# A fused attention and feed-forward kernel: adding transfers issued behind GpSimd's second long product, and new places for the pieces of the preparations

## The chip, the cores and the metric

The kernel runs on one core of a Trainium2 chip. The metric is the time of one execution on the device, in microseconds (us). The core has TensorE (PE, matrix products; PEld is its loading of weights), VectorE (DVE), ScalarE (ACT), GpSimd (POOL) and SyncE (SP, which only starts transfers here). GpSimd computes and also starts those transfers that add to what lies at their destination; writing out the descriptors of such a transfer keeps GpSimd busy.

## What is computed

Attention over pooled keys, and a feed-forward layer behind it:

```python
kv_pool = kv.reshape(B, H // r, r, W // r, r, C).mean(axis=(2, 4))   # r = 4
k = v = kv_pool.reshape(B, -1, C) @ w_sr                             # 768 keys
a = softmax((q @ k.T) / sqrt(C))
x = a @ v                                    # B = 4, N = 12288, C = 128
h = x @ w_in                                 # d_ff = 2048
out = (h - tanh(h)) @ w_out
```

Every output element of 4 x 12288 x 128 in float32 is wanted.

## The kernel before

The queries go in groups of 512: 24 groups in each of 4 batches, 96 in all. A group has an attention part (`attention`) and a feed-forward part (`feed_forward`). The attention is written about the centre of a batch's keys, so that only what lies beyond a linear term needs exp: three tiles of scores (line 774), E = exp of them (778, ScalarE), r2 = E - 1 - s (781, VectorE). The three r2 of a group are added into one tile rs by transfers: a plain copy from SP (794) and two adding transfers that GpSimd starts (797). The sum of rs gives the shares (802), den; the values (818) and three products of the straight term (808) give num; df = num x t (829) is rounded to dr (832, GpSimd), and what the rounding left is dl (858, GpSimd). ql (812, GpSimd) is the same for q.

The feed-forward part takes dr through eight pairs of products with a scaled w_in (889). For seven of the eight the cubic term is one square on ScalarE (893) and one operation on VectorE (896). For the first of the eight, GpSimd does it: ScalarE copies (900), GpSimd adds 1 (903) and multiplies twice (907): first z = z x v, then rp = z x v. These are GpSimd's two long products. The products with Wr (927) gather all eight and the slope's term (878) in acc, and line 938 copies the result out.

The order is not written out line by line. Each operation is given to a planner (`Plan`) with a step, an engine, a duration and the tiles that it reads and writes. A step is an eighth of a group (UN = 8), so that group g's feed-forward starts at step 8g. The places within a group are in the table AT; `more` = [6.92, 9.07] are the two long products. Operations marked `lane` keep the order of their steps on their engine. All others go where the planner's own simulation has them ready, the one with the lowest step first. Tiles with one tag share a ring of buffers in the order of the tiles' steps. The PSUM bank "x" is such a ring with one buffer: den, num and most of the small products of the preparations pass through it one after the other, with den at 0.46 and num at 1.98 modulo 8.

Ahead of batches 1 to 3 lies a preparation:

- The gathering: the 16 places of the pooling window are added into kvp (768 keys for each of 128 channels, 384 KB a transfer). SP loads the first (368), GpSimd starts the 15 others as adding transfers (366), one in each group. `GATHER` says how many groups before the batch's first group this begins.
- `keys`: partial sums of kvp on VectorE (428), their mean (432), the centre (440, 443), then kvp times w_sr twice (447, 456), the second moment (473) and its norm (346). They are `apart_by` steps apart.
- `about_centre`: the hidden layer at the centre (536, 541), a chain of small operations on GpSimd (561 to 592), and twelve pieces on GpSimd: four that scale winT for the slopes (678), four for Wr (698) and four that scale w_in (636). The slopes' products are at 685, in bank x. The tuples EARLY (batches 0 and 1) and LATER (2 and 3) hold their distances in steps: FS of the first products, CS of the chain's parts, AS of the slopes and the Wr pieces, APART from a slopes piece to its product, SA, TA and WI the starts of slopes, Wr and w_in, and WS the distance of the w_in pieces. Batch 0 reads none of the values that are changed.

Of the kernel before, what the change touches and what calls it, by code (L numbers as in the profile page):

```python
# [156 lines left out]
def attention_then_ffn(ctx: ExitStack, tc: tile.TileContext, q, kv_by_key, kv_by_place, w_sr, w_in,  # L157
                       w_out, out):
    nc = tc.nc
    V, A, PL, PE, SP = nc.vector, nc.scalar, nc.gpsimd, nc.tensor, nc.sync  # L160
# [5 lines left out]
    KH, UN, AN = K // 2, FT // 2, KT // 2  # L166
    NG = N // G
# [7 lines left out]
    plan = Plan(tc)  # L175
# [7 lines left out]
    def sb(key, tag, shape, dt=F32, step=-1e6):  # L183
        n = BUFS[tag]
        plan.tile(key, tag, n, lambda: wk.tile(shape, dt, tag=tag, name=tag, bufs=n), step)
# [169 lines left out]
    def keys(b, s0):  # L355

        kvp, row, cen, kTr, vv32, vvr, Mn = (
            f"{x}.{b}" for x in ("kvp", "row", "cen", "kTr", "vv32", "vvr", "Mn"))
# [4 lines left out]
        for w in range(W if b else 0):  # L363
            def gather(w=w):
                if w:
                    PL.dma_start(out=plan[kvp], in_=kv_by_place[b - 1, w], accum_op=ALU.add)
                else:
                    SP.dma_start(out=plan[kvp], in_=kv_by_place[b - 1, w])

            at = (b * NG - GATHER[b - 1] + max(w - 1, 0)) * UN + AT["more"][0] - 2 * UN  # L370
            plan.op(at - (0.01 if w else 4), *(("POOL", 0.87) if w else ("SP", 0.5)), gather, (), (kvp,),
                    late=3.0, dma=1.0, lane=w > 0)
        for j in range(0 if b else NK):
            gap = 0.1
# [2 lines left out]
            at = slice(j * KB, (j + 1) * KB)  # L377
# [24 lines left out]
        sb(Mn, "Mn", [P, C])  # L402
        Mh = f"Mh.{b}"
        sb(Mh, "Mh", [P, 2, C], R32)
        apart_by = (1, 5.3, 8, 8)[b]
        s1, s2, s3, s4 = (s0 + n * apart_by for n in range(1, 5))
        s4 = s4 if b else 24.0
        for x, at in ((pc, s0), (pm, s3), (p4, s4)):
# [95 lines left out]
    def about_centre(b, s0):  # L504
# [12 lines left out]
        sb(Wr, "Wr", [P, FT, C], R32)  # L517
        FS, CS, AS, APART, SA, TA, WI, WS = EARLY if b < 2 else LATER
        first_at = [s0 + FS * n if b else s0 - 9.9 + n / 4 for n in range(4)]
# [86 lines left out]
        if b:  # L606
            plan.op(known, on, 2.2, first_order, (hb,), (hb, gg), late=MORE)
            plan.op(known + CS, on, 1.9, slopes_of, (hb,), (hb,))
# [62 lines left out]
        for n in range(NW):  # L671
# [27 lines left out]

            plan.op(slopes_at[n], "POOL", 1.1, by_first, (gg, "winT"), ((wg, 0),), late=MORE if b else 0.0)  # L700
            plan.op(slopes_at[n], "ACT", 0.2, beside, (gg,), ((wg, 1),), late=0.1)
# [26 lines left out]
    AT = dict(  # L728
        forth=[3.94, 1.06, 1.67, 5.41, 0.16, 6.02, 6.63, -0.46],
        first=[4.44, 1.51, 2.12, 5.84, 0.59, 6.45, 7.06, -0.02],  # L730
        then=[6.19, 2.26, 3.01, 6.54, 1.52, 7.28, 8.03, 0.77],
        back=[11.04, 6.93, 7.24, 7.85, 6.32, 8.76, 9.37, 5.71],
        scores=[-20.66, -21.57, -19.38], exps=[-20.16, -21.13, -18.94],
        beyond=[-19.46, -20.25, -18.25], values=[-3.75, -5.26, -4.35],
        more=[6.92, 9.07],
        copied=-18.59, added=[-15.50, -11.66],
# [122 lines left out]

        plan.op(s0 + AT["lower_left"], "POOL", 1.29, lower_left, (df, dr), (dl,), lane=True)  # L860

    EARLY = (2, 4.4, 5, 3.5, 8, 15, 22, 8)
    LATER = (4, 9, 9, 7, 16, 34, 31, 9)
    MORE = 2
    ON_POOL = (0,)

    def feed_forward(g, s0):
# [277 lines left out]
    start(-LEAD - 80)  # L1145
    weights(-LEAD - 50, -LEAD - 60)
    plan.tile("held", "held", 1, lambda: None)
    GATHER = (24, 30, 30)
    KEYS, ABOUT = 104, 96
    KEYS1, ABOUT1 = 61, 60  # L1150
    SL = 6
# [4 lines left out]
    for b in range(B):  # L1156
        first = b * NG * UN
        keys(b, first - LEAD - (40, KEYS1, KEYS, KEYS)[b])
        if b == 0:
            out_weights(-17.7, -LEAD - 46)  # L1160
        about_centre(b, first - LEAD - (30, ABOUT1, ABOUT, ABOUT)[b])
        for g in range(b * NG, (b + 1) * NG):
            attention(g, g * UN - (PRO[g] if g < 3 else 0))
# [19 lines left out]
def build(shapes):  # L1183

    import concourse.bacc as bacc

    nc = bacc.Bacc("TRN2", target_bir_lowering=False, num_devices=1)
    ins = [
        nc.dram_tensor(f"in_{n}_dram", s, mybir.dt.from_np(d), kind="ExternalInput").ap()
        for n, (s, d) in shapes.items()  # L1190
    ]
    b, c, n = shapes["q"][0]
    out = nc.dram_tensor(_OUT, (c, b * n), F32, kind="ExternalOutput").ap()
    with tile.TileContext(nc) as tc:
        attention_then_ffn(tc, *ins, out)
    return nc
# [31 lines left out]
```

## Time and profile before

| | before |
| --- | --- |
| median of 3 runs | 1312.98 us (1312.15 to 1314.66) |
| the profiled execution | 1312.51 us |
| its span, first to last instruction | 1310.7 us |
| TensorE busy | 1267.8 us (97%) |
| VectorE busy | 1221.1 us (93%) |
| ScalarE busy | 1196.2 us (91%) |
| GpSimd busy | 1142.7 us (87%) |
| GpSimd's adding transfers into kvp | 45, 44.2 us |
| TensorE's load for rp, waiting for GpSimd | 33.1 us in 47 waits |

The shares of busy time lie close together and are averages over stretches with different limits, so the profile is read group by group. In a row of the order of time the first number is the start, the second the duration, then engine, line, operation, destination and sources; in brackets stands how long the engine was idle before it and for whom. Rows merge neighbours of one kind (x3 is three of them). Durations of GpSimd's instructions overlap a little; their ends are what others wait for.

### The profile page before, as it was taken

How to read it: one execution, taken by the hardware profiler on the slowest of the kernel's cores; microseconds unless marked ns; L12 is line 12 of the kernel's file. 1: busy time of each engine (PE TensorE's matmuls, PEld its weight loads, DVE VectorE, ACT ScalarE, POOL GpSimd, SP SyncE). 2: the span in 40 equal slices, each digit the busy share in tenths (PEclk: the TensorE clock that was granted, in tenths of full speed). 3: DMA queues.
4: the chain of work that ended last, by engine and by line, in shares of the span. 5: the costliest groups of instructions: out<-in, count | busy, mean ns of one | idle time of the engine just before them, and what ended most of it. 6: DMA issues, size and time to landing. Idle time of an engine off the chain costs nothing.

```text
span 1310.7 us, 17375 instructions
## 1 busy us (share of the span) xinstructions
PE 1267.8 (97%) x5520; PEld 888.8 (68%) x5520; DVE 1221.1 (93%) x1201; ACT 1196.2 (91%) x1423; POOL 1142.7 (87%) x969
## 2 busy tenths in 40 slices
PE   5899999999999999999999999999999999999997
PEld 3666666776666667767666666776766767667665
DVE  7789999898999998999999999899999999899996
ACT  4689999898999998999999999899999999899995
POOL 3578999899999997999999998899988888888896
PEclk9899999999999999999999999999999999999999
DMA  9165666545666654345666664344344444344431
GB/s 354 47 122 128 139 133 143 111 116 127 135 136 137 139 121 110 104 122 117 134 138 139 133 137 114 92 120 114 96 107 111 107 105 109 93 107 105 110 86 37
DMA packets 82708, 158.47 MB, mean 121 GB/s; under 512 B 9936, under 2 KB 12112, under 8 KB 82608
## 3 DMA queue, kind: packets, MB, share of 16 engines
q0 software_dynamic: 33552, 66.99, 31.4%
q1 hardware_dynamic: 49056, 90.29, 19.4%
q8 instruction: 45, 0.74, 0.2%
q14 instruction: 55, 0.45, 0.1%
HBM read 57.93 MB, written 25.39 MB: 64 GB/s over the span
## 4 chain that ended last, share of the span: by engine, by line
PE 42%; POOL 40%; ACT 8%; issue 5%; DVE 3%; DMA 2%; POOLq 0%; SPq 0%; ACTq 0%; DVEq 0%
PE acc L927 12%; PE big L889 11%; POOL rp L907 10%; POOL z L907 10%; POOL rs L797 5%; PE big L774 5%; PE x L818 4%; POOL z L903 4%; ACT E L778 4%; POOL dr L832 3%; POOL ql L812 3%; PE acc L878 2%; PE x L808 2%; ACT v L900 2%; ACT o L938 2%
## 5 line engine op out<-in xcount | busy, mean ns | idle before, releaser
L896 DVE SCALAR_TENSOR_TENSOR r<-big,u 128x1024 fp32r<-128x1024 f32 x672 | 778.4, 1217 | 24.9 <-ACT u L893 23.7
L893 ACT ACTIVATE u<-big 128x1024 f32<-128x1024 f32 x672 | 662.0, 1035 | 35.2 <-PE big L889 24.5
L889 PE MATMUL big<-dr,winr 128*128 128x512 f32 x1536 | 510.0, 413 | 1.6 <-DVE r L896 0.7
L927 PE MATMUL acc<-r,Wr 128*128 128x512 f32 x1344 | 426.1, 409 | 0.6 <-DVE r L896 0.6
L781 DVE SCALAR_TENSOR_TENSOR r<-E,big 128x1024 f16<-128x1024 f32 x288 | 350.2, 1217 | 41.1 <-ACT E L778 37.8
L889 PEld LDWEIGHTS big<-dr,winr 128*128 128x128 f32 x1536 | 276.8, 188 | 95.6 <-DVE r L781 23.5
L778 ACT ACTIVATE E<-big 128x1024 f32<-128x1024 f32 x288 | 296.1, 1029 | 16.4 <-PE big L774 6.0
L927 PEld LDWEIGHTS acc<-r,Wr 128*128 128x128 f32 x1344 | 251.7, 188 | 64.7 <-DVE r L896 1.5
L907 POOL TENSOR_TENSOR rp<-z,v 128x1024 fp32r<-128x1024 f32 x96 | 272.8, 2841 | 0.2
L907 POOL TENSOR_TENSOR z<-z,v 128x1024 f32<-128x1024 f32 x96 | 247.6, 2579 | 4.3
L797 POOL DMA_DIRECT2D rs<-r x188 | 222.0, 1181 | 5.9 <-DVE r L896 3.3
L774 PE MATMUL big<-qr,kTr 128*128 128x512 f32 x576 | 197.9, 425 | 4.4 <-ACT qr L759 1.6
L818 PE MATMUL x<-r,vvr 128*128 128x512 f16 x576 | 174.9, 386 | 0.0
L812 POOL TENSOR_TENSOR ql<-q,qr 128x512 fp32r<-128x512 f32 x96 | 163.3, 1701 | 5.2 <-ACT qr L759 5.2
L858 POOL TENSOR_TENSOR dl<-df,dr 128x512 fp32r<-128x512 f32 x96 | 163.7, 1706 | 0.0
L832 POOL TENSOR_SCALAR dr<-df 128x512 fp32r<-128x512 f32 x96 | 66.6, 694 | 108.5 <-DVE df L829 106.4
L774 PEld LDWEIGHTS big<-qr,kTr 128*128 128x128 f32 x576 | 105.0, 190 | 45.9 <-DVE r L781 15.0
L903 POOL TENSOR_SCALAR z<-v 128x1024 f32<-128x1024 f32 x96 | 107.8, 1123 | 0.0
L900 ACT COPY v<-big 128x1024 f32<-128x1024 f32 x96 | 97.8, 1018 | 1.1 <-PE big L889 1.0
L818 PEld LDWEIGHTS <-vvr 128*128 128x128 f16 x576 | 33.5, 98 | 79.4 <-issue 79.1
L938 ACT ACTIVATE o<-acc,At 128x512 f32<-128x512 f32 x96 | 65.7, 684 | 21.6 <-PE acc L927 21.4
L927 PE MATMUL acc<-rp,Wr 128*128 128x512 f32 x192 | 73.8, 466 | 10.8 <-POOL rp L907 7.7
(184 smaller groups left out, 1007.0 us busy)
## 6 DMA issues: line engine op xcount, KB each, us to landing
rs<-r POOLq DMA_DIRECT2D x188, 256.0 KB, 3.9
q<-in_q_dram SPq DMA_DIRECT2D x96, 256.0 KB
out_dram<-o SPq DMA_DIRECT2D x96, 256.0 KB
rs<-r SPq DMA_DIRECT2D x94, 256.0 KB
kvp<-in_kv_by_place_dram POOLq DMA_DIRECT2D x45, 384.0 KB, 5.0
r<-in_kv_by_key_dram SPq DMA_DIRECT2D x6, 512.0 KB
kc<-inverse SPq DMA_DIRECT2D x12, 256.0 KB
u<-in_moe_w_in_dram SPq DMA_DIRECT2D x3, 512.0 KB
```

Of the source, the lines that this page charges most:

```text
L774: PE.matmul(out=half(plan[s], h), lhsT=plan[kTr][:, n * P : (n + 1) * P], rhs=plan[qr], start=True, stop=True)
L778: A.activation(out=plan[e], in_=plan[s], func=AF.Exp)
L781: V.scalar_tensor_tensor(out=plan[r], in0=plan[e], scalar=-1.0, in1=plan[s], op0=ALU.add, op1=ALU.subtract)
L797: PL.dma_start(out=plan[rs], in_=plan[r2s[k]], accum_op=ALU.add)
L812: PL.tensor_tensor(out=plan[ql], in0=plan[qs], in1=plan[qr].bitcast(F32), op=ALU.subtract)
L818: PE.matmul(out=plan[num], lhsT=plan[vvr][:, n], rhs=half(plan[f"r2.{g}.{k}"], h), start=(start and h == 0), stop=(stop and h == 1))
L858: PL.tensor_tensor(out=plan[dl], in0=plan[df], in1=plan[dr].bitcast(F32), op=ALU.subtract)
L889: PE.matmul(out=half(plan[hp], h), lhsT=plan[winr][:, f * P : (f + 1) * P], rhs=plan[dr], start=True, stop=True)
L893: A.activation(out=plan[u], in_=plan[hp], func=AF.Square)
L896: V.scalar_tensor_tensor(out=plan[r], in0=plan[hp], scalar=1.0, in1=plan[u], op0=ALU.add, op1=ALU.mult)
L907: PL.tensor_tensor(out=plan[to], in0=plan[x], in1=plan[y], op=ALU.mult)
L927: PE.matmul(out=plan[acc], lhsT=plan[Wr][:, 2 * n + h], rhs=half(plan[r], h), start=(start and h == 0), stop=(stop and h == 1))
```

## The change

```diff
-            at = (b * NG - GATHER[b - 1] + max(w - 1, 0)) * UN + AT["more"][0] - 2 * UN
-            plan.op(at - (0.01 if w else 4), *(("POOL", 0.87) if w else ("SP", 0.5)), gather, (), (kvp,),
+            at = (b * NG - GATHER[b - 1] + max(w - 1, 0)) * UN + AT["more"][1] - 2 * UN
+            plan.op(at + (0.01 if w else -4), *(("POOL", 0.87) if w else ("SP", 0.5)), gather, (), (kvp,),
                     late=3.0, dma=1.0, lane=w > 0)
...
-        apart_by = (1, 5.3, 8, 8)[b]
+        apart_by = (1, 6, 8, 8)[b]
...
-    EARLY = (2, 4.4, 5, 3.5, 8, 15, 22, 8)
-    LATER = (4, 9, 9, 7, 16, 34, 31, 9)
-    MORE = 2
+    EARLY = (2.5, 4.4, 4, 6, 8, 18, 24, 8)
+    LATER = (4, 6, 9, 7, 18, 30, 31, 7)
+    MORE = 2.5
...
-    GATHER = (24, 30, 30)
+    GATHER = (24, 29, 29)
```

The adding transfers into kvp get a step just behind the second long product in place of one just ahead of the first. The first load by SP moves by the same 2.15 steps. For batches 2 and 3 the gathering begins one group later. In the preparation of batch 1 the parts of `keys` lie 6 steps apart in place of 5.3, the first products 2.5 in place of 2, the slopes' pieces 4 in place of 5 and their products 6 behind them in place of 3.5, and the pieces for Wr and w_in begin 3 and 2 steps later. In batches 2 and 3 the chain's parts lie 6 apart in place of 9, the slopes begin 2 steps later, the Wr pieces 4 sooner, and the w_in pieces lie 7 apart in place of 9. MORE is the time that the planner adds behind two operations in its simulation. No instruction is added or taken away.

## Rows read from the trace of the kernel before

**Rows 1.** Windows, line 938 only: stretch, length, busy (instructions), clock, DMA share, GB/s.

```profile
98.90:237.10 138.20, 7.57 (x12) 1.00 0.63 135
352.30:478.00 125.70, 6.94 (x11) 1.00 0.63 137
627.10:790.40 163.30, 8.96 (x14) 1.00 0.64 137
963.20:1085.50 122.30, 6.85 (x11) 1.00 0.44 108
```

**Rows 2.** Order of time, one group with an adding transfer into kvp.

```profile
406.11 0.61 POOL L832 TENSOR_SCALAR dr<-df 128x512 fp32r<-128x512 f32 x1 [1.06 <-DVE df L829]
...
407.69 0.87 POOL L366 DMA_DIRECT2D kvp<-in_kv_by_place_dram  x1
...
411.27 3.02 POOL L907 TENSOR_TENSOR rp<-z,v 128x1024 fp32r<-128x1024 f32 x1
...
413.65 1.88 POOL L858 TENSOR_TENSOR dl<-df,dr 128x512 fp32r<-128x512 f32 x1
...
414.34 0.30 PEld L927 LDWEIGHTS acc<-rp,Wr 128*128 128x128 f32 x2 [0.60 <-POOL rp L907]
...
416.11 1.49 POOL L797 DMA_DIRECT2D rs<-r  x1
...
422.74 0.60 PE L802 MATMUL x<-rs,share 128*128 128x512 f16 x2
```

**Rows 3.** Order of time, one group without such a transfer.

```profile
1027.86 0.62 POOL L832 TENSOR_SCALAR dr<-df 128x512 fp32r<-128x512 f32 x1 [1.54 <-DVE df L829]
...
1032.58 2.69 POOL L907 TENSOR_TENSOR rp<-z,v 128x1024 fp32r<-128x1024 f32 x1
...
1035.67 0.81 PE L927 MATMUL acc<-rp,Wr 128*128 128x512 f32 x2
...
1039.21 0.39 PE L878 MATMUL acc<-dl,Ah 128*128 128x512 f32 x1
```

**Rows 4.** Waits, 352 to 478 us: who waited for whom, total, times, longest.

```profile
PEld acc L927 <- POOL rp L907: 5.8, 10, 0.6
DVE r L781 <- ACT E L778: 4.5, 10, 0.9
```

**Rows 5.** Windows: PE, PEld, DVE, ACT, POOL busy; then line 366 alone.

```profile
282.40:352.30 69.90, 66.15 (x297) 46.75 (x296) 63.32 (x61) 61.46 (x76) 69.90 (x58) 1.00 0.60 130
...
282.40:352.30 69.90, 7.67 (x5) 1.00 0.60 130
```

**Rows 6.** Windows of the preparations of batches 1 to 3, line 938 only.

```profile
237.10:352.30 115.20, 5.43 (x9) 1.00 0.53 122
490.30:627.10 136.80, 6.84 (x11) 1.00 0.47 113
802.70:938.70 136.00, 6.90 (x11) 1.00 0.42 105
```

**Rows 7.** Order of time at the end of batch 2's gathering.

```profile
486.70 2.69 POOL L907 TENSOR_TENSOR rp<-z,v 128x1024 fp32r<-128x1024 f32 x1
...
492.54 0.17 DVE L432 TENSOR_REDUCE row<-row 128x1 f32<-128x24 f32 x1
...
498.99 0.60 PE L802 MATMUL x<-rs,share 128*128 128x512 f16 x2
```

**Rows 8.** Tiles kvp (100 to 480 us) and rs (350 to 480): landings.

```profile
DMA to landing us min/median/max: 4.6/5.1/6.3
...
DMA to landing us min/median/max: 3.8/3.9/4.5
```

**Rows 9.** Order of time in batch 1's preparation: the straight term behind a slopes piece.

```profile
295.19 0.30 PEld L808 LDWEIGHTS x<-qr,Mh 128*128 128x128 f32 x2 [1.18 <-DVE At L692]
295.20 0.73 PE L808 MATMUL x<-qr,Mh 128*128 128x512 f32 x2 [0.74 <-DVE At L692]
```

**Rows 10.** The page's DMA queues: kind, packets, MB, share of 16 engines.

```profile
q0 software_dynamic: 33552, 66.99, 31.4%
```

## The prediction

> **What bounds the kernel now.** I first cut the span into groups of 512 queries by the start of the result copy of line 938, which stands once in each group. Three stretches in which GpSimd begins one adding transfer per group last 138.20 us for 11 periods, 125.70 for 10 and 163.30 for 13; a late stretch with no such transfer lasts 122.30 for 10 [rows 1]. That is 12.56 us a group with the transfer and 12.23 without. These 34 groups are the largest piece of the span that the change touches, so the question is what the 0.33 us are.
>
> The order of time of one such group answers it [rows 2]. Counting from the start of dr at 406.11: the transfer's issue is at +1.58, before the first long product, and the second long product rp ends at 411.27 + 3.02 = 414.29, which is +8.18. TensorE's weight load for line 927 starts at 414.34, having waited 0.60 us for rp. In a group without the transfer [rows 3] rp ends at 1032.58 + 2.69 = 1035.27, which is +7.41 from dr at 1027.86, and TensorE takes it at 1035.67, +7.81, with no wait named. So the transfer pushes rp back by 8.18 - 7.41 = 0.77 us, of which 7.81 - 7.41 = 0.40 is free and some 0.37 is not: the 0.33 of the period. The list of waits says the same of ten groups: TensorE's loads for rp 5.8 us, and behind them VectorE for E 4.5 us [rows 4], because the scores stand behind rp in TensorE's order. Without the transfer VectorE has no such idle time, its work fills the 12.23 us, and this is the floor of a group.
>
> **Adding transfers behind the second product.** Fifteen issues per batch for batches 1 to 3 are moved past z*v, the first rs issue and rp on GpSimd's queue; nothing is added or removed. Their step is 0.01 after rp and 1.57 before dl (lower_left), and the lane fixes that order. rp then ends at +7.41 again, 0.40 before TensorE wants it. What is late next? Behind the transfer stand dl, ql, the second rs issue and the next dr. Their start doesn't move: the transfer was ahead of them before. dl ends at 413.65 + 1.88 = 415.53, +9.42 [rows 2], and TensorE takes dl at +11.35 [rows 3]: 1.9 us spare. The second rs issue ends at 417.60, +11.49, and dr is wanted at +12.23: GpSimd still waits 0.7 us for VectorE. So in the steady groups I cost the move at nothing, with these 0.7 us as the cover; a further 0.7 us of GpSimd work in such a group would bring the loss back. Gain: 138.20 + 125.70 + 163.30 - 34 x 12.23 = **11.4 us**, bounds 6 (if half of the wait comes back elsewhere) and 11.4.
>
> **One group later for batches 2 and 3** (29 in place of 30). In the preparation of batch 1 GpSimd is full for 69.9 us on end with five issues in it [rows 5]; four of them stay, behind rp. One issue less is 0.8 us. The three preparations take 115.20 us for 8 periods, 136.80 for 10 and 136.00 for 10 [rows 6], so above the floor 17.4, 14.5 and 13.7 us. The third has no adding transfer in it, the second had two at its end, and these go: 14.5 - 13.7 = 0.8 us. Together **1.6 us**, bounds 0.5 and 2.
>
> **The end of the gathering gets tight.** The last transfer of batch 2 was issued ahead of group 30's first product; now it is behind rp of group 31, at about 489.1 of the old time [rows 7]. It lands 4.6 to 6.3 us after its issue, median 5.1 [rows 8], so at 493.7 to 495.4. The six partial sums (line 428, about 0.2 us each) and the mean, which stood at 492.54, need it: the mean moves to 495 to 497. The planner reckons with a landing 4.87 us after the issue (0.87 + 3.0 + 1.0 in the code) and puts these small operations accordingly, but VectorE and TensorE take their queues in order: if the transfer lands later, up to 6.3 - 4.9 = 1.4 us of VectorE's queue (the cubes, then TensorE, which waits for them) stand behind it. The group's shares, which need the same PSUM bank after the centre, are at 498.99 [rows 7], so 2 us remain for the centre. The same holds for batch 3. In batch 1 the last issue moves only behind group 12's rp, about 5.6 us later, and lands just before its sums' old place. Besides, partial sums that slipped into VectorE's idle time of a transfer group find none now. Loss: 0 to 1.4 for each of three batches and up to 0.3 for the sums; I take 0.5 each, **1.5 us**, bounds 0 and 4.
>
> **Places of the preparation's pieces.** In batch 1 the second slopes piece had a place, 131.5 + 5 = 136.5, which modulo 8 is 0.5: between the shares (0.46) and the straight term (1.98), which use the same bank x. TensorE idled 0.74 us there, its load 1.18 [rows 9]. The new places (129.5 + 6 + 4n: 7.5 and 3.5 modulo 8) lie outside. But the moment of batch 1 goes from 126.9 to 129.0, which is 1.0 modulo 8, inside: TensorE's 12 products are work anyway, ScalarE's copy behind them is not, and no row shows it in this place; by the wait at [rows 9] I bound its cost by 0 and 1.2 us and take 0.6, as its input is ready early, which the slopes' was not. With the rest of batch 1's excess over batch 3 (17.4 - 13.7 = 3.7 us, of which the issues explain some 0.8 already booked and four that stay some 3) this leaves **0.6 us** gain, bounds -2 and 2.5. In batches 2 and 3 the pieces come in another order (chain 3 and 6 steps sooner, Wr 4 sooner, slopes 2 later, first slopes at 3 in place of 1 modulo 8). TensorE and VectorE have that work to do in any order, and idle gaps before dr take the pieces as soon as they are ready; I take 0, bounds -1.5 and 1.5 for both together. If a piece falls before rp and finds no idle time, a 0.8 us transfer's price (0.33) or more comes back in that group alone.
>
> **Sum.** 11.4 + 1.6 - 1.5 + 0.6 = 12.1 us. The profiled execution took 1312.51 us, its span 1310.7 with 1.8 around it; it gives 1300.4. The median of the runs shown is 0.47 above that execution, so I say 1300.9.
>
> **Rivals.** (1) *The steady gain comes, the rest turns against it*: late landings at their upper bound (4), pieces at theirs (-3.5), no gain from the later start: 11.4 + 0.5 - 4 - 3.5 = 4.4, so 1308.5. For it: the 2 us left for the centre; against: bounds seldom meet. Chance 0.10. (2) *Another wait takes rp's place*, since the 0.40 us of spare time at rp and the 0.7 us at dr are thin and the second rs issue now has the transfer just ahead of it: half of the steady gain, 1312.9 - 6.4 = 1306.5. Against it: a group without the transfer runs the very same order to the end of rp. 0.06. (3) *The move changes nothing*: the wait named for rp is in truth one for VectorE, which is as full either way (0.99 of the floor). Then only the pieces count, 1312 to 1313. Against: the waits vanish together with the transfer. 0.03.
>
> (4) *Slower: the shares wait.* Adding transfers for kvp and rs go out on one software queue: 45 x 0.393 + 188 x 0.262 MB is the 66.99 MB of queue 0 [rows 10]. So far the first rs transfer ran behind kvp's, now the second does, and it has no further transfer to wait for it but the shares. It is issued at +10.0 [rows 2], 2.9 after kvp's new issue at +7.1, and the shares are at 422.74, +16.63, or +16.3 at the shorter period: 6.3 us. If it moved only once kvp has landed, it would land at 5.1 - 2.9 + 3.9 = 6.1 in the median, just in time, but 6.3 - 2.9 + 3.9 = 7.3 at worst. The point is a landing of kvp's over 5.3 us; with half the transfers 0.9 late, 45 groups lose 20 us and the 11.4 are gained: 1312.9 + 9 = 1322. Against it: rs transfers issued 2.97 us behind kvp's land in 4.5 us at most, 3.9 in the median [rows 8]. Chance 0.03. The Trainium skill, page "DMA: Bandwidth & Descriptors", section "Two DMAs through the same engine are not ordered", says that on one queue of one DMA engine descriptors start in order but are pipelined. By its first half the second rs transfer would stand behind all of kvp's, as in this rival; by its second half it overlaps, and the trace agrees with that, with 4.5 us at most.
>
> **How the numbers follow.** Forecast 0.78, rivals 0.10, 0.06, 0.03 and 0.03. The best end of all bounds, 11.4 + 2 - 0 + 2.5 + 1.5 = 17.4, gives 1295.5; the upper end has to take in rival 2 and most of rival 1: 1307.5. A measurement of this kernel can tell some 0.2%, 2.6 us, from no change. Faster by more: 0.78 + 0.06 + most of 0.10 = 0.92; within: 0.04; slower: 0.04, rival 4 and a preparation that goes wrong by more than all the rest gains.
>
> **What would show it.** In the changed profile: periods of 12.2 to 12.3 us in groups with a transfer, no wait of line 927 for rp and none of VectorE for E there, the transfer's issue between rp and dl, GpSimd's idle time before dr 0.6 to 0.8 us (step one); the preparations of batches 1 to 3 at about 15, 14 and 14 us above the floor (steps two and four); partial sums in one run, and a wait of VectorE's line 428 or TensorE's line 440 of up to 1.4 us at the end of each gathering (step three). I am wrong if the period stays at 12.5, if the shares (line 802) wait for a transfer, or if a stretch outside the gathering grows by more than 4 us.

## The result and the profile after

| | before | after |
| --- | --- | --- |
| median of 4 runs each, side by side | 1313.68 us (1312.15 to 1314.66) | 1299.28 us (1297.68 to 1302.0) |
| ratio to before, 95% interval | | 0.9894 [0.987, 0.9917] |
| span of the profiled execution | 1310.7 us | 1300.2 us |

The forecast was 1300.9 us, 1.6 us above the median that came. The stretches below are read from single executions, and the profiled one of the changed kernel is the slowest of its four (1302.0 us): between the two profiles lie 10.5 us, between the medians 14.4. Some of the forecast's terms came out otherwise than it said, and one was missing. First the changed kernel's profile, in the order of the rows of before.

Windows of line 938 alone in the changed kernel: first the three steady stretches with a transfer in each group (11, 10 and 13 periods) and the late one without (10), as in [rows 1]; then the three preparations of [rows 6] (8, 10 and 10 periods). Columns: stretch, length, busy (instructions), granted clock, DMA share, GB/s.

```profile
96.60:231.50 134.90, 7.46 (x12) 1.00 0.62 136
345.90:469.15 123.25, 6.83 (x11) 1.00 0.65 139
620.50:779.90 159.40, 8.87 (x14) 1.00 0.65 140
950.50:1072.80 122.30, 6.80 (x10) 1.00 0.44 108
231.50:345.90 114.40, 5.44 (x9) 0.99 0.51 119
481.80:620.50 138.70, 6.82 (x11) 0.99 0.44 109
792.10:928.10 136.00, 6.84 (x11) 1.00 0.44 108
```

The periods with a transfer are 12.26, 12.33 and 12.26 us, where [rows 1] gave 12.56; without one 12.23, as before. The steady stretches are 3.3, 2.4 and 3.9 us shorter, together 9.6. The second preparation has become longer, 138.70 for 136.80, which the third stretch's gain must not hide.

Order of time of one steady group of the changed kernel, to be laid beside [rows 2, 3]; 394.21 belongs to the group ahead.

```profile
394.21 1.16 POOL L366 DMA_DIRECT2D kvp<-in_kv_by_place_dram  x1
...
398.65 0.47 SPq L794 DMA_DIRECT2D rs<-r  x1
...
399.32 0.62 POOL L832 TENSOR_SCALAR dr<-df 128x512 fp32r<-128x512 f32 x1 [0.54 <-DVE df L829]
...
403.41 0.87 POOL L797 DMA_DIRECT2D rs<-r  x1
...
404.05 2.68 POOL L907 TENSOR_TENSOR rp<-z,v 128x1024 fp32r<-128x1024 f32 x1
...
406.42 1.16 POOL L366 DMA_DIRECT2D kvp<-in_kv_by_place_dram  x1
...
407.09 0.41 PEld L927 LDWEIGHTS acc<-rp,Wr 128*128 128x128 f32 x2
...
408.29 1.85 POOL L812 TENSOR_TENSOR ql<-q,qr 128x512 fp32r<-128x512 f32 x1
...
409.51 1.48 POOL L797 DMA_DIRECT2D rs<-r  x1
...
411.53 0.61 POOL L832 TENSOR_SCALAR dr<-df 128x512 fp32r<-128x512 f32 x1 [0.54 <-DVE df L829]
```

The issue stands behind rp. rp ends at 406.73, +7.41 from dr, to the hundredth as in the group without a transfer, and TensorE takes it at 407.09 with no wait named. GpSimd waits 0.54 us ahead of dr: that is what is left of its spare time. The second rs issue ends at 409.51 + 1.48 = 410.99, +11.67 from dr, where the prediction had +11.49. The copy by SP and the first rs issue stand here because they turn out to matter below: the copy begins 4.4 us behind the transfer into kvp, and the first rs issue, 4.76 us behind the copy, waits for nothing.

The waits of the changed kernel between 345 and 470 us (who waited for whom: total, times, longest), as in [rows 4]:

```profile
PEld acc L927 <- POOL rp L907: 1.8, 2, 0.9
DVE r L781 <- ACT E L778: 1.5, 2, 0.7
```

TensorE's 5.8 us for rp are 1.8, VectorE's 4.5 us for E are 1.5. The rest is in the first groups of the stretch, where a piece that scales w_in stands behind the transfer: it uses up GpSimd's idle time, and the next group's rp is 0.89 us late.

The end of batch 2's gathering in the changed kernel, in order of time, as in [rows 7]:

```profile
480.61 1.18 POOL L366 DMA_DIRECT2D kvp<-in_kv_by_place_dram  x1
...
486.25 1.25 DVE L428 TENSOR_REDUCE row<-kvp 128x4 f32<-128x128 f32 x6 [1.03 <-DMA kvp<-in_kv_by_place_dram]
...
488.69 0.73 PE L889 MATMUL big<-dr,winr 128*128 128x512 f32 x2 [2.10 <-DVE r L781]
...
490.65 1.05 PE L889 MATMUL big<-dr,winr 128*128 128x512 f32 x2
...
494.26 0.63 PE L889 MATMUL big<-dr,winr 128*128 128x512 f32 x2
```

The six partial sums stand in one run. VectorE waits 1.03 us for the last transfer, and r2 (781) stands behind the sums; so TensorE idles 2.10 us. Behind that idle time the same pair of products takes 1.05 us where it takes 0.63 at 494.26: the granted clock has fallen. The last stretch of this section shows it, this group in the changed kernel and then in a second run of the same kernel (`e4_again`); columns: stretch, length, busy of PE, PEld, DVE, ACT and POOL, granted clock, DMA share, GB/s.

```profile
481.80:497.90 16.10, 14.00 (x55) 9.80 (x54) 13.41 (x20) 13.04 (x15) 14.04 (x11) 0.89 0.53 114
```

```profile
480.20:494.70 14.50, 12.61 (x55) 8.81 (x54) 12.98 (x20) 12.80 (x15) 14.02 (x11) 1.00 0.55 118
```

The second run has nearly the same waits here (0.83 us for kvp, 1.89 us of idle TensorE) but kept the clock, and its group is 1.6 us shorter. There the clock fell at the end of batch 3's gathering instead, where a group of 15.7 us has a mean granted clock of 0.89.

### The profile page after: what moved, and what is told of

Same layout as the page of the kernel before. It is cut to its first block, busy times and chain, and to the rows that moved or that the text cites. A ratio compares the mean times of both kernels' runs of the same rounds, so it can differ in the third digit from the quotient of the medians.

```text
span 1300.2 us, 17380 instructions
## 1 busy us (share of the span) xinstructions
PE 1260.9 (97%) x5520; PEld 887.4 (68%) x5520; DVE 1219.9 (94%) x1201; ACT 1193.4 (92%) x1423; POOL 1147.6 (88%) x969
## 4 chain that ended last, share of the span: by engine, by line
PE 65%; POOL 23%; issue 4%; DMA 4%; DVE 2%; ACT 2%; SPq 0%; POOLq 0%; DVEq 0%; ACTq 0%
PE big L889 19%; PE acc L927 19%; PE big L774 8%; PE x L818 7%; POOL rp L907 5%; POOL z L907 4%; PE x L808 4%; PE acc L878 3%; POOL rs L797 3%; PE x L802 2%; POOL ql L812 2%; POOL dr L832 2%; POOL z L903 2%; DMA rs<-r 1%; POOL dl L858 1%
## 5 line engine op out<-in xcount | busy, mean ns | idle before, releaser
L907 POOL TENSOR_TENSOR rp<-z,v 128x1024 fp32r<-128x1024 f32 x96 | 257.1, 2679 | 0.2
L907 POOL TENSOR_TENSOR z<-z,v 128x1024 f32<-128x1024 f32 x96 | 231.8, 2415 | 7.9
L797 POOL DMA_DIRECT2D rs<-r x188 | 204.2, 1086 | 7.4 <-DMA rs<-r 6.2
L774 PE MATMUL big<-qr,kTr 128*128 128x512 f32 x576 | 193.8, 418 | 2.3 <-DVE r L781 0.8
L832 POOL TENSOR_SCALAR dr<-df 128x512 fp32r<-128x512 f32 x96 | 70.6, 736 | 88.5 <-DVE df L829 84.7
L774 PEld LDWEIGHTS big<-qr,kTr 128*128 128x128 f32 x576 | 101.8, 188 | 49.0 <-DVE r L781 26.5
L903 POOL TENSOR_SCALAR z<-v 128x1024 f32<-128x1024 f32 x96 | 111.8, 1165 | 0.0
L938 ACT ACTIVATE o<-acc,At 128x512 f32<-128x512 f32 x96 | 65.4, 682 | 12.2 <-PE acc L927 11.7
```

The source lines that it names most:

```text
L774: PE.matmul(out=half(plan[s], h), lhsT=plan[kTr][:, n * P : (n + 1) * P], rhs=plan[qr], start=True, stop=True)
L797: PL.dma_start(out=plan[rs], in_=plan[r2s[k]], accum_op=ALU.add)
L907: PL.tensor_tensor(out=plan[to], in0=plan[x], in1=plan[y], op=ALU.mult)
```

## Experiments

For every run the times of the result copy of line 938 were read, so that a difference can be put to a stretch. "Start" is the first such copy; "steady" are the 34 periods of [rows 1]; "end 2" and "end 3" are the three groups in which the gathering for batches 2 and 3 ends and the preparation begins. From one profile each, us:

| | start | steady | preparation 1 | end 2 | end 3 |
| --- | --- | --- | --- | --- | --- |
| before | 82.3 | 427.1 | 115.3 | 40.9 | 40.9 |
| after | 80.0 | 417.5 | 114.4 | 44.2 | 41.4 |
| e4_again (after once more) | 80.0 | 417.4 | 112.7 | 42.7 | 43.3 |
| e1_move_only | 80.0 | 416.7 | 115.3 | 41.2 | 41.1 |
| e2_pieces_only | 83.8 | 427.8 | 114.0 | 40.8 | 40.8 |
| e3_gather_30 | 79.7 | 417.4 | 113.7 | 41.9 | 41.1 |
| e8_first_three | 79.7 | 427.4 | 115.3 | 40.9 | 40.8 |

**Is it the move?** The kernel before with the new place behind rp, and all else as it was:

```diff
-            at = (...) * UN + AT["more"][0] - 2 * UN
-            plan.op(at - (0.01 if w else 4), ...
+            at = (...) * UN + AT["more"][1] - 2 * UN
+            plan.op(at + (0.01 if w else -4), ...
```

> The kernel before with the place behind the second long product alone; GATHER, the tuples and apart_by stay as they were. Theory: the wait for rp in the steady groups is the change's whole worth. 34 or 35 groups go from 12.56 to 12.23 us (11.3 us), and the start up to the first result copy stays about 2 us shorter, as in the changed kernel (80.0 against 82.3 us), since the first issue no longer stands among batch 0's pieces: 1300 us, 1298 to 1302. Rival: the places of the pieces bring a part, and without them batch 1's preparation is worse than before by the transfers that now stand behind rp: 1303 to 1306.

Measured: 1299.66 us, ratio 0.9894 [0.9879, 0.9909]. The third of its steady stretches (the others are 134.95 and 122.30), window of line 938:

```profile
617.90:777.30 159.40, 8.84 (x14) 1.00 0.65 140
```

The move alone is as fast as the whole change. It gains 10.4 us in the steady stretches and 2.4 in the start.

**And the rest without it?** The changed kernel with the old place and with 30 groups of lead:

```diff
-            at = (...) * UN + AT["more"][1] - 2 * UN
-            plan.op(at + (0.01 if w else -4), ...
+            at = (...) * UN + AT["more"][0] - 2 * UN
+            plan.op(at - (0.01 if w else 4), ...
...
-    GATHER = (24, 29, 29)
+    GATHER = (24, 30, 30)
```

> The changed kernel with the adding transfers ahead of the first long product again and GATHER at 30: only the tuples and apart_by are new. Theory: the steady groups are at 12.56 us again, each with a wait for rp of 0.6 us, and the pieces move time only within the preparations: 1311 to 1315 us. Rival: the pieces have a share of their own in the gain: 1310 or less, and the three preparations together shorter by 3 us or more.

Measured: 1311.03 us, ratio 0.9982 [0.9972, 0.9993]. The waits between 353 and 478 us are the old ones:

```profile
PEld acc L927 <- POOL rp L907: 5.4, 9, 1.1
DVE r L781 <- ACT E L778: 5.0, 11, 0.9
```

Of the 2.3 us that it seems to gain, its profile has 1.2 in the preparation of batch 1 and 0.7 in that of batch 3. Another 1.7 lie behind the last preparation, where the two kernels don't differ in any step. The windows of 1119 to 1131 us, before and then this run, show why (columns as in the last windows above):

```profile
1119.00:1131.00 12.00, 9.22 (x34) 6.05 (x33) 7.81 (x8) 7.85 (x10) 10.52 (x12) 0.86 0.42 96
```

```profile
1119.00:1131.00 12.00, 9.26 (x40) 6.41 (x40) 8.95 (x9) 8.99 (x11) 10.63 (x12) 1.00 0.39 89
```

TensorE idles as long in both, and in one of them the granted clock fell. Against that the start is 1.5 us later here, and the second steady stretch 0.5 us longer. The interval puts the whole at 1 to 4 us, part of it the clock's; in the preparations the pieces are worth about 2 us.

**The later gathering.** The changed kernel with 30 groups of lead for batches 2 and 3, and beside it the changed kernel once more:

```diff
-    GATHER = (24, 29, 29)
+    GATHER = (24, 30, 30)
```

> The changed kernel with GATHER at 30 for batches 2 and 3, so that the last transfer lands a group before its sums. Theory: the 3.3 us that batch 2 loses in the three groups at the end of its gathering (44.2 us against 40.9 before) come from VectorE's wait for the last landing; here they are gone, no partial sum waits for a transfer, and one more issue each in the preparations of batches 1 and 2 costs 0.8 us: 1297 to 1298.5 us in the median. Rival: the loss is the partial sums' work and the order around it, not the landing: 1299 to 1301 us, with those three groups still over 43 us.

> The changed kernel once more, on the same chip as the three others. Its four runs so far lie between 1297.7 and 1302.0 us. Theory: what differs between them is when the last transfers land; the steady periods are 12.22 to 12.25 us again, and the three groups at the end of batch 2's gathering differ from the 44.2 us of the first trace whenever the landing does. Rival: the run's length is set elsewhere: those groups take 44.2 us again, whatever the run's time.

Measured: 1297.92 us, ratio 0.9889 [0.9873, 0.9904], for 30 groups; 1299.34, ratio 0.9887 [0.987, 0.9904], for the changed kernel again. The times can't be told apart. The stretches can: with 30 groups line 428 waits for nothing, and the two ends take 41.9 and 41.1 us, where with 29 they take 44.2 and 41.4, or 42.7 and 43.3. The eight groups behind them take 107.6 and 106.8 us with 30, 107.2 and 106.8 with 29. One group later costs 2.5 to 3.0 us at the two ends together and gives back 0.3 to 0.6 behind them. Each run with 29 has one drop of the clock, worth 1.6 us, in these 2.5 to 3.0. The preparation of batch 1, which has one issue less with 29, takes 114.4 and 112.7 us with it and 113.7 without.

**How thick is the cover?** In groups 44 to 53 and 68 to 77 ql is computed twice; the first of these have a transfer, the others none.

```diff
+            for _ in range(2 if 44 <= g < 54 or 68 <= g < 78 else 1):
-            PL.tensor_tensor(out=plan[ql], ...
+                PL.tensor_tensor(out=plan[ql], ...
```

> The changed kernel with ql (line 812) computed twice in 10 groups with an adding transfer (44 to 53) and in 10 groups without one (68 to 77): the same 1.24 us of GpSimd work more in each, in the same order. Theory: GpSimd's idle time before dr is the cover of the move, 0.56 us with the transfer and 1.50 without. Then the first ten lose 1.24 - 0.56 = 0.68 us each (periods of 12.9) and the last ten nothing (12.23): 6 to 7.5 us in all, 1305 to 1308. Rival: GpSimd's time doesn't set the period in either, and both stay at 12.23 (1299), or the order behind rp hurts by itself and both lose alike.

Measured in one run: 1309.01 us, 1 us above the theory's range. The stretch that was 159.40 us long, its waits, and two rows of a group (line numbers stand one higher here: 928 is 927, 908 is 907):

```profile
618.90:786.80 167.90, 8.89 (x14) 1.00 0.63 133
```

```profile
PEld acc L928 <- POOL rp L908: 11.1, 10, 1.6
...
DVE r L781 <- ACT E L778: 9.8, 11, 1.5
```

```profile
672.66 3.25 POOL L813 TENSOR_TENSOR ql<-q,qr 128x512 fp32r<-128x512 f32 x2
...
676.46 0.93 POOL L833 TENSOR_SCALAR dr<-df 128x512 fp32r<-128x512 f32 x1
```

The two ql last 3.25 us where one lasted 1.85, so the added work is 1.4 us and not the 1.24 that was expected. Ten groups pay 8.5 us: nine of them 0.80 each, and the first 1.33, in which a piece of the preparation already uses the idle time. So about 0.6 us was covered in a steady group. That is GpSimd's idle time ahead of dr (0.54 to 0.58 us in the changed kernel), and here dr has no wait any more; the loss comes back through the same door, rp. Nine of the ten groups without a transfer keep 12.2 us; the first, which has such a piece as well, takes 13.11 in place of 12.25. The prediction's 0.7 us of cover was a little too thick, the mechanism was right.

**Between the two long products.** The changed kernel with the transfer just behind z*v, ahead of the first rs issue and rp:

```diff
-            at = (...) * UN + AT["more"][1] - 2 * UN
+            at = (...) * UN + AT["more"][0] - 2 * UN
```

> The changed kernel with the adding transfer between the two long products: behind z*v, still ahead of rp. Theory: only what stands ahead of rp counts, and rp ends at +8.18 from dr again: periods of 12.56 with a wait for rp of 0.6 us, 1309 to 1312 us. Rival: it is the distance to the rs transfers or to the first product that mattered; then the periods are 12.23 and the time 1298 to 1300.

Measured: 1319.22 us, ratio 1.0043 [1.0028, 1.0058], above what the theory gave. Waits between 352.6 and 480.8 us:

```profile
PEld acc L927 <- POOL rp L907: 8.2, 10, 1.6
...
POOL rs L797 <- DMA rs<-r: 4.7, 6, 1.1
```

rp is pushed back as before the change (its end is at +8.30 from dr, median), and on top GpSimd itself now waits for transfers: the first rs transfer, directly behind kvp's in the queue, lands late (the rs tile's landings are 3.3 to 7.5 us, 5.1 in the median, for [rows 8] 3.8 to 4.5), and the second adding transfer into the same tile waits for it. This is the mechanism of the rival with the slower result, on another transfer than it named.

**Behind the second rs issue.** If only GpSimd's work ahead of rp counted, the last place of the order would be as good:

```diff
-            at = (...) * UN + AT["more"][1] - 2 * UN
+            at = (...) * UN + AT["added"][1]
```

> The changed kernel with the adding transfer behind the second rs issue, at the end of GpSimd's work before the wait for dr, one place earlier in time (4.7 steps) than in the changed kernel. Theory: still nothing of it is ahead of rp within a group, since the wait for dr takes it: periods of 12.23. The second rs transfer is ahead of it on the queue and lands in 3.6 to 3.9 us again, in place of 3.9 to 6.4; kvp's last landing is 7 us sooner, so no partial sum waits for it and TensorE doesn't idle there: 1296.5 to 1298.5 us. Rival: GpSimd's 0.56 us before dr are no cover for an issue that ends just then, dr is late, and the periods are 12.4 or more: 1303 or more.

Measured: 1340.57 us, ratio 1.0199 [1.0176, 1.0222]. Both expectations miss. Order of time of one group, then the waits between 363.6 and 497.1 us:

```profile
418.61 1.50 POOL L366 DMA_DIRECT2D kvp<-in_kv_by_place_dram  x1
...
419.60 0.47 SPq L794 DMA_DIRECT2D rs<-r  x1
...
425.81 0.89 POOL L797 DMA_DIRECT2D rs<-r  x1 [1.40 <-DMA rs<-r]
```

```profile
POOL rs L797 <- DMA rs<-r: 13.8, 9, 1.7
PEld acc L927 <- POOL rp L907: 13.5, 10, 1.6
```

The copy that begins a group's rs is issued 1.0 us behind the transfer into kvp, and the first adding transfer, which needs the copy, gets going only 6.2 us after it. In the changed kernel that distance is 4.76 us without a wait. GpSimd stands still for 1.4 us, with rp behind it in its order. The theory that formed here: a transfer into kvp that flies beside SP's copy delays the copy, and through the first rs issue it delays rp. In 32 of the 34 steady groups there is such a wait, 1.54 us in the median; less the 0.40 that rp has to spare, this gives 12.23 + 1.14 = 13.37 us, and the measured periods are 13.34, 13.35 and 13.35.

**One instruction later.** If so, the place behind rp is good only because the copy comes late enough after it. Behind dl the transfer begins 1.3 us nearer to the copy:

```diff
-            at = (...) * UN + AT["more"][1] - 2 * UN
+            at = (...) * UN + AT["lower_left"] - UN
```

> The changed kernel with the adding transfers into kvp issued one instruction later, behind dl in place of behind rp. GpSimd's order is then dr, z*v, first rs issue, rp, dl, transfer, ql, second rs issue. Theory: only what the transfer pushes back counts. In the changed kernel dl has some 1.9 us to spare either way, the second rs issue has the same work ahead of it, so the steady periods stay at 12.2 to 12.3 us and the time is 1297 to 1302 us. Rival, from the run with the transfer behind the second rs issue: a transfer into kvp that flies beside the plain copy of the next rs or beside the second rs transfer delays them. The transfer begins 1.3 us nearer to both, so the first rs issue (line 797) would wait for the copy, or the shares (line 802) for the second rs transfer, by some 0.3 to 0.8 us in each of the 34 steady groups: 1308 to 1325 us.

Measured: 1330.16 us, ratio 1.0111 [1.0085, 1.0137], beyond even the rival's range. Order of time of one steady group, then the waits between 638.6 and 806.4 us:

```profile
690.22 1.19 POOL L366 DMA_DIRECT2D kvp<-in_kv_by_place_dram  x1
...
693.02 0.47 SPq L794 DMA_DIRECT2D rs<-r  x1
...
698.22 0.59 PE L802 MATMUL x<-rs,share 128*128 128x512 f16 x2 [0.29 <-DMA rs<-r]
...
699.07 0.89 POOL L797 DMA_DIRECT2D rs<-r  x1 [1.25 <-DMA rs<-r]
```

```profile
POOL rs L797 <- DMA rs<-r: 12.8, 12, 1.5
```

The copy begins 2.8 us behind the transfer, and the first rs issue waits in 29 of the 34 steady groups, 1.00 us in the median of these: 12.23 + 1.00 - 0.40 = 12.83, measured 12.79, 13.06 and 12.91. The shares wait too, up to 0.5 us for the second rs transfer, in 9 of the 13 groups of this stretch. So one place later in GpSimd's order costs 31 us: 22 in the steady stretches, the rest mostly in the preparation of batch 1 and at the ends of the gatherings. The change as made stands 1.3 us from that.

The copy's own landing stands in the traces as the sixteenth update of its semaphore. Counted from the copy's issue, in the median of the steady groups, it comes after 2.7 us before the change (no transfer into kvp in flight), 3.5 in the changed kernel, 5.2 with the transfer behind dl and 5.8 with it behind the second rs issue. Where the first rs issue waits, it begins 0.55 us after the landing. It comes up in GpSimd's order 4.75 us behind the copy, so in the changed kernel the copy has some 0.7 us to spare, and the one steady group that waits (0.35 us) is the one whose copy landed latest (4.6). The Trainium skill, page "DMA: Bandwidth & Descriptors", section "Issuing engines are not separate DMA queues", says that transfers end up on the same 16 DMA engines and interleave there, whichever engine started them. The traces agree: SP's copy lands the later, by 1.7 us in the median here, for transfers that GpSimd started.

**Is it the transfer's size?** The order of the kernel behind the second rs issue, but each transfer adds only half of the keys:

```diff
-                    PL.dma_start(out=plan[kvp], in_=kv_by_place[b - 1, w], accum_op=ALU.add)
+                    PL.dma_start(out=plan[kvp][:, 0:K // 2], in_=kv_by_place[b - 1, w][:, 0:K // 2], accum_op=ALU.add)
```

> The kernel with the adding transfers behind the second rs issue (it took 1340.6 us, periods 13.1 to 14.1), but each of the 45 transfers adds only the first half of the 768 keys (192 KB in place of 384); the adding of the other half of the pooled keys is left out. The number and the places of all instructions are the same, and the issue still writes descriptors for 128 channels. Theory: the length of the transfer in flight beside the plain copy of rs delays that copy, and with it the first rs issue and rp. With half the length the wait of the first rs issue (line 797) for the copy falls from 1.3 to 2.5 us to under 0.8, the steady periods to 12.3 to 12.8, the time to 1300 to 1318 us. Rival: it is not the length but the place in the order (the issue itself, or a fixed cost of every adding transfer beside the copy): the wait stays over 1.2, the periods at 13 or more, the time at 1330 to 1342 us.

Measured: 1301.9 us, ratio 0.9911 [0.9894, 0.9928]. Order of time of one group:

```profile
670.63 1.49 POOL L366 DMA_DIRECT2D kvp<-in_kv_by_place_dram  x1
...
672.01 0.47 SPq L794 DMA_DIRECT2D rs<-r  x1
...
676.87 0.89 POOL L797 DMA_DIRECT2D rs<-r  x1
```

The copy is issued 1.4 us behind the transfer, and the first rs issue follows 4.86 us later with no wait; of the 34 steady groups five wait, 0.15 to 0.60 us. All three steady stretches are back at 12.26, 12.34 and 12.26 us. Issue, order and place are those of the 1340.6 us kernel, so what costs there is how much the transfer carries. That it is in flight at all is not enough: the half transfer still takes 5.3 us to land (5.0 to 5.5), most of it beside the copy. The copy is delayed by the half too: it lands 4.1 us after its issue in the median, for 5.8, which is just inside what the first rs issue leaves it. It begins 0.4 us later behind the transfer than there, but in the four groups where it begins 1.0 to 1.1 us behind it lands in 4.2 to 4.6, so the distance is not the reason.

**The start.** Nothing in the prediction touches the time before the first group, yet it is 2.3 us shorter. The kernel before, with the new place for the first three adding transfers alone:

```diff
+            if b == 1 and 0 < w < 4:
+                at += AT["more"][1] - AT["more"][0] + 0.02
```

> The kernel before with the new place for the first three adding transfers of batch 1 alone, those that run beside batch 0's preparation. Theory: the first result copy comes at about 80 us in place of 82.3 to 83.8, as in all kernels with the new place, since the first issue stood among batch 0's slopes pieces; all later stretches are as before: 1309.5 to 1311.5 us. Rival: the start differs between runs only by the clock that TensorE is granted there: 82 to 84 us again, and 1312 to 1314.

Measured: 1310.84 us, ratio 0.9987 [0.9977, 0.9998], and its start is at 79.7 us. GpSimd's order of time, before and then this run (its lines stand two higher):

```profile
45.54 1.01 POOL L366 DMA_DIRECT2D kvp<-in_kv_by_place_dram  x1
46.36 2.26 POOL L678 TENSOR_TENSOR Wg<-winT,hb 128x512 f32<-128x512 f32 x2
...
54.13 2.04 POOL L678 TENSOR_TENSOR Wg<-winT,hb 128x512 f32<-128x512 f32 x2
...
60.67 0.62 POOL L832 TENSOR_SCALAR dr<-df 128x512 fp32r<-128x512 f32 x1 [0.55 <-DVE df L829]
```

```profile
45.37 3.22 POOL L680 TENSOR_TENSOR Wg<-winT,hb 128x512 f32<-128x512 f32 x3
...
58.36 0.62 POOL L834 TENSOR_SCALAR dr<-df 128x512 fp32r<-128x512 f32 x1
58.93 1.02 POOL L366 DMA_DIRECT2D kvp<-in_kv_by_place_dram  x1
```

The first issue stood among batch 0's slopes pieces. With it gone from there, three of the four pieces go out together, the third at about 47.5 us in place of 54.1, and the first dr follows 2.3 us sooner; the issue stands behind it. With the transfers behind rp or behind dl the start is at 79.7 to 80.0 us in every run; between the products it is at 81.1, behind the second rs issue at 84.5.

## Why the prediction was right, and where it was not

**The steady groups** were the term that decided, 11.4 us of 12.1. The reading of [rows 2, 3] holds: with the transfer gone from ahead of rp, rp ends at +7.41, and the waits for rp and for E vanish but for the first groups of a stretch. Measured 10.4 us with the move alone and 9.6 in the changed kernel's profile, inside the bounds; with the transfer ahead of rp again, between the products (`e6_between`), the gain is gone. The difference to 11.4 is in part a single group of 13.20 us in the changed kernel, the first of the second stretch, where a w_in piece behind the transfer uses up the cover and rp is late by 0.89 us. The prediction had named such a case (a piece that finds no idle time) without booking it.

**The cover** was named rightly, the idle time ahead of dr, but sized 0.7 us where 0.54 to 0.58 shows and `e5_ql_twice` could use about 0.6. The step that was off is "their start doesn't move": the end of the second rs issue moved from +11.49 to +11.67, since the issue takes 0.95 us behind rp (406.73 to 410.99 is 4.26 us, in [rows 2] 414.29 to 417.60 is 3.31) and 0.77 ahead of it.

**What is late next** is the step that was wrong, though the sum didn't suffer. It went through GpSimd's queue (dl, ql, second rs issue, dr) and found spare time everywhere. It didn't ask which other transfer begins while the moved one is in flight: the next group's copy by SP. This copy, not the second rs transfer of the fourth rival, is the one that makes the kernel slower, and the point from which it decides is less than 1.3 us from the chosen place. The rival's chance of 0.03 was argued from rs transfers behind kvp's of [rows 8], so from the adding queue alone; and the 4.5 us at most that it rested on holds for 350 to 480 us, over all three stretches of before it is 6.0. Its mechanism is real: `e6_between` shows it on the first rs transfer, and in `e9_behind_dl` the shares wait. In the changed kernel they wait twice, 0.7 us in all, and in no steady group.

**The start** was left out: 2.3 us. The prediction looked for the moved issues in the steady groups and in the preparations of batches 1 to 3, and the first one stands in neither: it was ahead of the first group, among batch 0's pieces.

**The later gathering** was booked at +1.6 us and gave 0.6 at most. One half was counted twice: the two transfers at the end of the second preparation cost what they cost because they stood ahead of rp, and the move had already taken that away (with the move alone the second and third preparations take 136.6 and 136.4 us, 0.2 apart in place of 0.8). It was misread too: "these go" holds for one of the two only, the other is still issued in that preparation, at 619.3 us. The other half, one issue less where GpSimd is full in batch 1's preparation [rows 5], doesn't show: that stretch is 115.3 us before and with the move alone, and with 29 or 30 groups of lead it is as long within what the clock changes (one group of it is 16.1 us at a granted clock of 0.89 in the changed kernel and 14.5 at 1.00 in its second run).

**The tight end** was booked at -1.5 us, for three batches. The wait was foreseen well (1.03 and 0.83 us, bound 1.4), what follows it was not: TensorE idles twice as long as VectorE waits, since r2 stands behind the sums, and the clock may fall after it. Measured 2.5 to 3.0 us for two batches against 30 groups of lead, within the bounds of 0 to 4, and 1.6 of it is a drop of the clock that came once in each of the two runs. Batch 1's end has no such wait for kvp, and batch 3's has one in the second run alone (0.57 us). So the second preparation came out 16.4 us above the floor where the prediction had 14; the first has 16.6 for 15, the third 13.7 for 14.

**The pieces** were booked at +0.6; they gave about 2 us in the preparations of `e2_pieces_only`, of which 0.5 came back there, and 1.0 in the changed kernel's group of 13.20 us. The wait of [rows 9] is gone.

So the start (+2.3, not booked) and the three terms that were too good (1 to 2 us of the steady term, 1 of the gathering, 1 to 1.5 of the tight end) nearly cancel, and that the total came so close is in part luck. These terms add up to about the 10.5 us between the two profiles; where the rest of the 14.4 between the medians lies isn't shown; one drop of the clock in a single group alone is worth 1.6 us. The rivals that needed a new wait in place of rp's had 0.06 and 0.03; the place shows that they deserved more, since the trace of before couldn't exclude them.

Two things stay open. The last group of the gathering waits for its copy in the changed kernel (0.81 and 0.92 us in the two batches) and in the kernel with 30 groups (1.51), though the copy begins as late behind the transfer as in the steady groups, and with the move alone it doesn't. The traces point at a third party, the queue that the profile calls "instruction" (q8). While the first of these copies flew, from 471.98 to 477.1 us, the changed kernel's DMA view has one packet of it, of 16 KB and 1.4 us:

```profile
q8 instruction: 1, 0.02, 1.7%
```

In the four profiles with the transfer behind rp (`after`, `e4_again`, `e1_move_only`, `e3_gather_30`) 175 copies begin within 6 us of a transfer into kvp. The 155 without such a packet beside them land within 4.7 us; of the 20 with one, nine take 5.1 to 5.8, all the waits named here among them, and eleven no longer than the others, the one with the move alone (4.5) among them. No run varies the packet, so the cause is argued and not shown. And no version here is told apart from the changed kernel as faster: the one with 30 groups, 1297.92 us, is so by less than the intervals.

## What to carry to other kernels

An instruction that starts a transfer has two places, the one on the engine that issues it and the one in time in which its bytes move; moving it off the path of the first says nothing of the second. List for the new place every other transfer that begins until the moved one has landed (some 5 us here), on other queues too, and who waits for those with how much to spare. And when a periodic step is moved, look up its first and last instances by themselves: here they gave the largest unbooked gain and the worst-sized loss.

## What the hardware showed that was not expected

- A 384 KB adding transfer from HBM delays a 256 KB copy on another queue by an amount that turns on the distance between them and on its size. The copy lands 3.5 us after its issue when it begins 4.5 us behind the transfer, 5.2 at 2.8 us and 5.8 at 1.0 us; with 192 KB at 1.4 us it is 4.1, and 2.3 where no transfer into kvp runs at all (medians of the steady stretches and of the late one). The second rs transfer flies beside the copy too, in each place at another distance, so only 5.8 and 4.1, from one place in the order, tell of the size by itself.
- The transfer itself lands in 5.2 us behind rp, 5.9 behind dl and 6.6 behind the second rs issue (medians of steady stretches). With half the bytes it still takes 5.3.
- After about 2 us in which TensorE idled, the mean granted clock of the group was 0.89 in one execution and 1.00 in another of the same kernel, with the same waits; pairs of products took 1.05 us in place of 0.63. It cost 1.6 us in that group. The same shows at 1119 to 1131 us: alike idle time, 0.86 in one kernel and 1.00 in the other, and 1.7 us between the two stretches.
